# Other column order for the hidden layer, w2 loaded in four parts, conditional sums moved, first gates split

## The chip, the cores and the metric

The kernel runs on one core of one Trainium2 chip. The metric is the device time in microseconds (us) of one execution. The five instruction streams of a core are named as the profile names them: PE (TensorE, with PEld for its weight loads), DVE (VectorE), ACT (ScalarE), POOL (GpSimd) and SP (SyncE). SP computes nothing here: it reads numbers into registers and issues most of the DMAs, one after the other, in program order.

## What is computed

Chunked attention (8 batches, 8 heads, 576 positions, head size 64, chunks of 64) feeds a layer of 8 experts, of which each token uses one:

```
out   = softmax(scale * q_c @ k_c.T) @ v_c          # per chunk of 64, all float32
x     = out as (4608, 512)
xn, en = x and expert_emb, each row over its norm
p     = softmax(xn @ en.T / tau)                    # 8 experts
e     = argmax(p)
h     = relu(x @ w1[e])                             # w1: (8, 512, 1024)
y     = p[e] * (h @ w2[e])                          # w2: (8, 1024, 512)
```

## The kernel before

**Two stages.** The first 190 us or so are attention and routing, in 36 blocks of 128 tokens. Each token's row goes to a place in a DRAM table (`spots`) that is sorted by expert. The rest is the expert layer. It works in steps `j`, each on two groups of 64 tokens: group 0 comes from the experts counted upwards from 0, group 1 from the experts counted downwards from 7. So each step uses two experts at a time, and an expert is changed in one group every nine steps or so.

**One step of the expert layer.** In the loop over `j`, PE does the hidden layer of step `j + 1` (`hidden_fast`) and then the last product of step `j` (`result`, 64 matmuls with 512 columns, line 413).
- `hidden_fast` multiplies in the manner of Strassen and Winograd: seven products p1 to p7 (line 342, 16 matmuls each) into PSUM, with sums of x made by DVE (`add_x`, line 318), sums of w1 kept in `sums` (`add_up`, line 291), and DVE adding the products up in `C` (line 374). ACT applies ReLU (`relu`, line 361), DVE turns the result around in 32x32 blocks (`turn`, line 368), and that is `hT`, which `result` of the next iteration reads. PSUM has six banks for the products, taken in turn.
- The hidden layer's 1024 columns are handled as 4 blocks `r` of 256 columns `x`. Before the change `x = 8 i + k`: i (32 values) becomes the partition of `hT`, k (8 values) its slice. ReLU therefore reads with a step of 8 elements (`"p (i k) -> p k i"`) and writes contiguously. w2 lies in SBUF as `w2_rows`, with partition `p = 32 r + i` holding rows `8 p` to `8 p + 7`: 16 KB in one piece per partition.
- `hidden_plain`, with `hidden_part` (lines 253, 263, 268), is the plain product, used in the first three steps and the last one.
- `gate_parts` computes the gate of a step with small operations on ACT and DVE (lines 224 to 234); it is a generator, and each `next` issues a part.

**What SP issues in each iteration**, in this order: `load_x(j + 5)` (two register loads, then four DMAs for rows of x and two of 4 KB), `load_w2(next_of(j))` (line 177; for each group two register loads, then one DMA of 2 MB with a condition: it moves data only where the expert is a new one for that buffer), and `load_behind(j + 2)` (the same for w1, into `next_w1`). `w2` has two buffers, so `load_w2(j + 2)` waits until `result(j)` has read the buffer. A conditional DMA is issued in every iteration, whether or not it moves data, and `result` waits for it.

**Change of expert.** `take_next` (line 299) reads, for each group, a flag into a register of DVE and one of ACT; if it is set, ACT copies three quarters of `next_w1` to `w1` (line 301) and DVE makes the four sums anew (line 291). `swap_next` calls it at the end of `hidden_fast`.

The program has an order written out by hand: each engine does its instructions in the order in which the code issues them. The functions that the change touches:

Of the kernel before, what the change touches and what calls it, by code (L numbers as in the profile page):

```python
# [12 lines left out]
AF = mybir.ActivationFunctionType  # L13
# [12 lines left out]
def kernel(  # L26
# [70 lines left out]
    spot = keep.tile([P, SPOTS, MW], FP32, name="spot")  # L97

    w1_rows = moe_w1.rearrange("e (p c) f -> p e (c f)", c=KD)
    w2_rows = moe_w2.rearrange("e (p c) d -> p e (c d)", c=KF)  # L100

    src_row = keep.tile([P, NST], I32, name="src_row")

# [17 lines left out]
    def whole(w):  # L121
        return w.rearrange("p c f -> p (c f)").unsqueeze(1)

    def load_first(buf, rows):

        for s in range(2):
            e = (0, E - 1)[s]
            nc.sync.dma_start(out=whole(buf[s]), in_=rows[:, e : e + 1, :], max_dma_last_dim=4096)

# [49 lines left out]
    def load_w2(j):  # L181
        for s in range(2):
            at = of_step(s, j)
            load_when(w2_sb[s][buf_of(j)], w2_rows, eblk[at], fresh[at])

    def load_behind(j):

# [49 lines left out]
    def hidden_part(j, s, b, w1, pool, tag, ps=None):  # L237

        d = mo[j]
        if b == 0:
            if ps is None:
                ps = pool.tile([P, G // Q, KF * Q], FP32, tag=tag, name="h_ps")
            d["ps"] = ps
            if s == 0:
                d["hT"] = bp.tile([P, KF, P], FP32, tag="hT", name="hT", bufs=2)
        ps, hT = d["ps"], d["hT"]
        w = w1[s].rearrange("p c (r x) -> p c r x", r=P // Q)
        t0 = G * s + Q * b  # L250
        for c in range(KD):
            for r in range(P // Q):
                nc.tensor.matmul(
                    ps[Q * r : Q * r + Q, b],
                    lhsT=d["xT"][:, c, t0 : t0 + Q],
                    rhs=w[:, c, r],
                    start=(c == 0),
                    stop=(c == KD - 1),
                )
        if b == G // Q - 1:  # L260
            h = bp.tile([P, G // Q, KF * Q], FP32, tag="h", name="h", bufs=1)
            for b in range(G // Q):
                nc.scalar.activation(
                    h[:, b].rearrange("p (k i) -> p k i", i=Q),
                    ps[:, b].rearrange("p (i k) -> p k i", i=Q),
                    AF.Relu,
                )
            nc.vector.transpose(
                hT[:, :, G * s : G * s + G].rearrange("p k (b i) -> p b k i", i=Q),
                h.rearrange("p b (k i) -> p b k i", i=Q),  # L270
            )
# [56 lines left out]
    def hidden_fast(j, ps_h, gate, turn_next, swap_next):  # L328

        d = mo[j]  # L330
        x = quarters(d["xT"])
        s1, s2, s3, s4 = d["S"]
        W2 = KF * Q

        def product(a, m):
            ps = bank(ps_h, [P, W2])
            for c in range(KD // 2):
                for s in range(2):
                    w = block(s, m)[:, c].rearrange("p (r x) -> p r x", r=2)
                    for r in range(2):  # L340
                        t0 = G * s + Q * r
                        nc.tensor.matmul(  # L342
                            ps[t0 : t0 + Q],
                            lhsT=a[:, c, s],
                            rhs=w[:, r],
                            start=c == 0,
                            stop=c == KD // 2 - 1,
                        )
            return ps


        last = "_last" if j == LEAST - 1 else ""
        hT = bp.tile([P, KF, P], FP32, tag="hT" + last, name="hT", bufs=1 if last else 2)
        d["hT"] = hT
        C = late_p.tile([P, 4, W2], FP32, tag="C", name="C")
        U, c11, c12, c22 = (C[:, i] for i in range(4))
        h = [late_p.tile([P, 2, W2], FP32, tag=f"h{b}", name=f"h{b}") for b in range(2)]

        def relu(b, v, x):
            for s in range(2):  # L360
                nc.scalar.activation(  # L361
                    h[b][G * v : G * v + G, s].rearrange("p (k i) -> p k i", i=Q),
                    x[G * s : G * s + G].rearrange("p (i k) -> p k i", i=Q),
                    AF.Relu,
                )

        def turn(b):
            nc.vector.transpose(  # L368
                hT.rearrange("p k (s b i) -> p b s k i", b=2, i=Q)[:, b],
                h[b].rearrange("p s (k i) -> p s k i", i=Q),  # L370
            )

        def add(out, a, b, op=ALU.add):
            nc.vector.tensor_tensor(out, a, b, op)  # L374

        p1 = product(x[:, 0, 0], "B11")
        nc.scalar.copy(U, p1)
        next(gate, None)
        next(gate, None)
        p2 = product(x[:, 1, 0], "B21")  # L380
        add(c11, U, p2)
        next(gate, None)
        relu(0, 0, c11)
        turn_next()
        p3 = product(s4, "B22")
        p5 = product(s1, "T1")
        p6 = product(s2, "T2")
        add(U, U, p6)
        add(c12, U, p5)
        add(c12, c12, p3)  # L390
        relu(0, 1, c12)
        for _ in gate:
            pass
        p7 = product(s3, "T3")
        add(U, U, p7)
        add(c22, U, p5)
        relu(1, 1, c22)
        p4 = product(x[:, 1, 1], "T4")
        swap_next()
        add(U, U, p4, ALU.subtract)  # L400
        relu(1, 0, U)
        turn(0)
        turn(1)
# [42 lines left out]
    with (  # L446
# [565 lines left out]
        for t in range(-3, NT + 3):  # L1012

            if 0 <= t < NT:
                turn_a(t)
            if t == early_t - 1:
                count_early()
            if t + 3 < NT:
                turn_qk(t + 3)
                if t + 7 < NT:  # L1020
                    load_qk(t + 7)
            if 0 <= t - 2 < NT:
                logits(t - 2)
            if t - 2 in ends:
                copy_logits(ends[t - 2])
            if t == NT:
                turn_x(t - 1)
            early_parts(t, 0)
            if 0 <= t + 2 < NT:
                scores(t + 2)  # L1030
            if t - 3 in ends:
                place(ends[t - 3])
            if 0 <= t - 1 < NT - 1:
                turn_x(t - 1)
            if 0 <= t < NT:
                values(t)
                b = (2 * t + 2) // NCB + 1
                if b not in v_t and b < B:
                    load_v(b)
            if t == NT - 8:  # L1040
                load_first(w1_sb, w1_rows)
            if t == NT - 6:
                load_first([w[0] for w in w2_sb], w2_rows)
            if 0 <= t + 2 < NT:
                weights(t + 2)
            if t - 2 in ends:
                pick(ends[t - 2])
            if early_t <= t < early_t + XBUF:
                load_early(t - early_t)

            put(1 if t < NT - 2 else 2)
            if t == NT - 3:
                turn_xb(0)
                load_early(XBUF)
            if t == NT - 1:
                turn_xb(1)
            early_parts(t, 1)
            if t == -2:
                turn_experts()
            if t == -1:  # L1060
                clear_first()
# [26 lines left out]
    with (  # L1088
# [10 lines left out]
                if behind_it is not None:  # L1099
                    behind_it(s)  # L1100

        def first_parts():
            for g in first_gates:
                next(g, None)

        first_parts()
        for j in range(LEAST - 1):
            n = j + 2

            def turn_next():  # L1110
                if n < LEAST:
                    turn_xb(n)
                    if n + XBUF < NJ:
                        load_x(n + XBUF)
                    add_x(n)

            def swap_next():
                if NE <= n < LEAST:
                    take_next(n)

            if j == 0:
                first_parts()
                add_up(0, None, TS)
                first_parts()
            elif j == 1:
                turn_next()
                add_up(1, None, TS)
                hidden_plain(2, w1_sb, lambda s: add_up(s, None, ("T3",)))
            else:
                gate = gate_parts(n) if n < LEAST else iter(())  # L1130
                hidden_fast(j + 1, ps_h, gate, turn_next, swap_next)

            result(j, ps_y)
            if NE <= next_of(j) < NJ:
                load_w2(next_of(j))
            if NE - 1 <= n < LEAST - 1:
                load_behind(n)
            elif n == LEAST - 1:
                load_late(LEAST)
# [73 lines left out]
```

## Time and profile before

| | us |
|---|---|
| time, median of 3 runs (lowest to highest) | 687.28 (686.48 to 689.08) |
| the profiled execution: its time | 686.3 |
| its span, first to last instruction | 684.5 |
| PE busy | 643.0 (94%) |
| ACT busy | 441.5 (65%) |
| DVE busy | 423.5 (62%) |
| POOL busy | 160.5 (23%) |
| ReLU in `relu` (L361), 264 of 677 ns | 178.8 |
| last product (L413), 2368 matmuls | 274.4 |
| seven products (L342), 3696 matmuls | 332.8 |

The profile is of one execution; sums from it are made against its own 684.5 us. "Idle before" names the engine that ended a wait. SP has no busy time in it, since register loads and DMA issues aren't counted, so its state has to be read from the timeline and the records of its queue ("SPq"). L177 is the line of the conditional weight loads.

### The profile page before, as it was taken

Reading aid. Unit: us, or ns where it says so; the run is one execution under the profiler, and the core shown is the slowest. Engines: PE = TensorE matmul, PEld = TensorE weight load, DVE = VectorE, ACT = ScalarE, POOL = GpSimd, SP = SyncE. Lnnn points to the kernel's source line nnn. Section 1 sums busy time; section 2 is a strip of 40 time slices with the busy share of each in tenths; the row PEclk is TensorE's granted clock in tenths of the full one; section 3 lists DMA queues with packets and bytes.
Section 4 is the critical chain, followed back from the end, with each engine's and each line's share of the span. In section 5 each row is a group of like instructions: output and inputs, shape, how many; then the busy total and the mean of one; then the engine's idle time right before and its main releaser. Section 6 shows DMA issues by size and latency. Waiting matters only on the chain. (4 is left out here: it accounts for less than half of the span.)

```text
span 684.5 us, 24832 instructions
## 1 busy us (share of the span) xinstructions
PE 643.0 (94%) x9735; PEld 363.4 (53%) x9735; DVE 423.5 (62%) x1139; ACT 441.5 (65%) x767; POOL 160.5 (23%) x245
## 2 busy tenths in 40 slices
PE   6699999999998989999999999999999999999991
PEld 4599999987543434544544444344444444444430
DVE  3378888878389554556576556767655665654520
ACT  4366666655224666767787777778777677777640
POOL 8747676742241000000100100001001000001001
PEclk9799999999999999999999999999999999999996
DMA  8969998989826811111777111775821115311110
GB/s 224 262 174 243 270 263 264 265 234 337 332 96 245 323 54 44 50 47 36 283 288 287 42 49 45 276 281 204 334 79 52 39 44 189 142 38 33 49 34 30
DMA packets 92670, 112.66 MB, mean 165 GB/s; under 512 B 50316, under 2 KB 70540, under 8 KB 92536
## 3 DMA queue, kind: packets, MB, share of 16 engines
q1 hardware_dynamic: 80552, 72.32, 33.2%
q0 software_dynamic: 11952, 38.56, 17.0%
q8 instruction: 81, 1.33, 0.8%
q14 instruction: 53, 0.43, 0.2%
q10 hardware_dynamic: 32, 0.02, 0.0%
HBM read 334.71 MB, written 22.69 MB: 522 GB/s over the span
## 5 line engine op out<-in xcount | busy, mean ns | idle before, releaser
L413 PE MATMUL y_ps<-w,hT 128*32 128x512 f32 (+1 forms) x2368 | 274.4, 587 | 2.3 <-DVE C L374 2.1
L361 ACT ACTIVATE h<-C 64x256 f32<-64x256 f32 x264 | 178.8, 677 | 93.2 <-DVE C L374 68.1
L413 PEld LDWEIGHTS y_ps<-w,hT 128*32 128x32 f32 x2368 | 87.5, 110 | 159.6 <-issue 145.6
L428 POOL DMA_INDIRECT out_dram<-y,spot x36 | 34.9, 968 | 436.0 <-ACT y L421 191.4
L374 DVE TENSOR_TENSOR C<-C,h 128x256 f32<-128x256 f32 x231 | 96.1, 416 | 46.7 <-DVEq L299 39.7
L342 PE MATMUL h<-w,S 128*32 128x256 f32 x1056 | 101.1, 380 | 2.0 <-DVE w L291 2.0
L342 PE MATMUL h<-sums,xbT 128*32 128x256 f32 x1056 | 101.1, 383 | 0.0
L342 PE MATMUL h<-w,xbT 128*32 128x256 f32 x1056 | 80.7, 380 | 6.4 <-ACTq L299 5.2
L368 DVE STREAM_TRANSPOSE hT<-h 128x512 f32<-128x512 f32 x66 | 46.7, 708 | 45.4 <-ACT h L361 45.3
L342 PEld LDWEIGHTS h<-w,xbT 128*32 128x32 f32 x1056 | 40.3, 110 | 43.1 <-ACTq L299 12.8
L342 PEld LDWEIGHTS h<-w,S 128*32 128x32 f32 x1056 | 48.0, 110 | 25.2 <-DVE w L291 1.5
L342 PEld LDWEIGHTS h<-sums,xbT 128*32 128x32 f32 x1056 | 48.4, 111 | 22.5 <-issue 0.8
L680 ACT COPY xT<-tr 128x512 f32<-128x512 f32 x36 | 21.1, 585 | 53.3 <-PE tr L678 53.3
L227 DVE TENSOR_SCALAR rn<-rn 128x1 f32<-128x1 f32 x37 | 5.7, 153 | 72.8 <-ACT rn L224 72.8
L342 PE MATMUL h<-sums,S 128*32 128x256 f32 x528 | 49.9, 379 | 0.0
L789 POOL DMA_INDIRECT spots<-xr,dest x36 | 37.0, 1029 | 39.3 <-ACT aT L637 13.0
L203 DVE STREAM_TRANSPOSE xbT<-xin 128x256 f32<-128x256 f32 x73 | 44.2, 644 | 0.5 <-DVE hT L368 0.5
L224 ACT ACT_TABLE_LOAD x34 | 43.6, 1283 | 0.9 <-issue 0.4
L231 ACT ACT_TABLE_LOAD x34 | 43.6, 1283 | 0.6
L421 ACT ACTIVATE y<-y_ps,gate 128x512 f32<-128x512 f32 (+1 forms) x37 | 25.2, 682 | 29.0 <-issue 12.8
L690 PEld LDWEIGHTS rt_ps<-enT,xT 128*128 128x128 f32 x288 | 35.0, 192 | 1.1 <-issue 0.8
L570 POOL DMA_DIRECT2D kx<-in_k_dram x36 | 31.6, 881 | 16.0 <-PE tr L593 15.2
(199 smaller groups left out, 846.6 us busy)
## 6 DMA issues: line engine op xcount, KB each, us to landing
w<-in_moe_w_dram SPq DMA_DIRECT2D x74, 2048.0 KB
next_w<-in_moe_w_dram SPq DMA_DIRECT2D x67, 2048.0 KB
xin<-spots SPq DMA_DIRECT2D x158, 64.0 KB
qx<-in_q_dram POOLq DMA_DIRECT2D x32, 256.0 KB, 6.0
v<-in_v_dram SPq DMA_DIRECT2D x56, 144.0 KB
kx<-in_k_dram POOLq DMA_DIRECT2D x28, 256.0 KB, 4.3
spot<-spots SPq DMA_DIRECT2D x80, 4.0 KB
spots<-blank SPq DMA_DIRECT2D x2, 576.0 KB
```

Of the source, the lines that this page charges most:

```text
L203: nc.vector.transpose(xT[:, :, cols].rearrange("p c (b i) -> p b c i", i=Q), t[:, s * (D // 2) : (s + 1) * (D // 2)].rearrange("p (b i c) ...
L224: nc.scalar.activation(rn, spot[:, j % SPOTS, SQ : SQ + 1], AF.Sqrt)
L231: nc.scalar.activation(sh, sh, AF.Exp, accum_out=gate)
L342: nc.tensor.matmul(ps[t0 : t0 + Q], lhsT=a[:, c, s], rhs=w[:, r], start=c == 0, stop=c == KD // 2 - 1,)
L361: nc.scalar.activation(h[b][G * v : G * v + G, s].rearrange("p (k i) -> p k i", i=Q), x[G * s : G * s + G].rearrange("p (i k) -> p k i", i=Q),
L368: nc.vector.transpose(hT.rearrange("p k (s b i) -> p b s k i", b=2, i=Q)[:, b], h[b].rearrange("p s (k i) -> p s k i", i=Q),)
L374: nc.vector.tensor_tensor(out, a, b, op)
L413: nc.tensor.matmul(ps[Q * r : Q * r + Q, 0:w], lhsT=d["hT"][:, c, Q * t0 : Q * t0 + Q], rhs=w2_sb[s][buf_of(j)][:, c, d0 : d0 + w], start= ...
L428: ins = nc.gpsimd.indirect_dma_start(out=to, out_offset=bass.IndirectOffsetOnAxis(ap=at, axis=0), in_=y[:, 0:w], in_offset=None, bounds_ch ...
L570: eng.dma_start(out=x[done : done + n], in_=src[b, :, s : s + n, :].rearrange("h p d -> p h d"),)
L690: nc.tensor.matmul(rt_ps[:, batch_of[t][0] % 2, batch_of[t][1]], lhsT=d["xT"][:, c], rhs=enT[:, c], start=(c == 0), stop=(c == KD - 1),)
L789: ins = nc.gpsimd.indirect_dma_start(out=spots, out_offset=bass.IndirectOffsetOnAxis(ap=at, axis=0), in_=m, in_offset=None, bounds_check=S ...
```

## The change

1. The columns of the hidden layer are ordered `x = 32 k + i` in place of `8 i + k`. ReLU reads and writes contiguously. In `hidden_part` two calls of 256 columns become one of 512.
2. So that the rows of w2 stand in the same order, w2 is loaded otherwise: partition `32 q + i`, slice `k` holds row `256 q + 32 k + i`. One DMA of 128 partitions becomes four of 32 partitions, each with eight rows of 2 KB per partition. This holds for the first load and for `load_w2`, where each of the four DMAs has the condition.
3. In `hidden_fast`, p4 is issued straight after p7, and `swap_next` straight after p4, ahead of the two additions that use p7 and of the ReLU behind them.
4. Before, the remaining parts of the first four gates were issued together ahead of and in iteration 0. Now the first gate is finished in iteration 0, and the parts of the other three stand in iteration 1, among the sums of w1.

```diff
-    w2_rows = moe_w2.rearrange("e (p c) d -> p e (c d)", c=KF)
+    w2_rows = moe_w2.rearrange("e (q k i) d -> q i e k d", k=KF, i=Q)
...
+    def load_first_w2():
+        for s in range(2):
+            e = (0, E - 1)[s]
+            for q in range(P // Q):
+                nc.sync.dma_start(
+                    out=w2_sb[s][0][Q * q : Q * q + Q].unsqueeze(1),
+                    in_=w2_rows[q, :, e : e + 1],
+                )
...
     def load_w2(j):
         for s in range(2):
             at = of_step(s, j)
-            load_when(w2_sb[s][buf_of(j)], w2_rows, eblk[at], fresh[at])
+            e, f = number(eblk[at], E - 1, ENG.SP), number(fresh[at], 1, ENG.SP)
+            for q in range(P // Q):
+                nc.sync.dma_start(
+                    out=w2_sb[s][buf_of(j)][Q * q : Q * q + Q].unsqueeze(1),
+                    in_=w2_rows[q, :, ds(e, 1)],
+                    cond=f > 0,
+                )
...
-            for b in range(G // Q):
-                nc.scalar.activation(
-                    h[:, b].rearrange("p (k i) -> p k i", i=Q),
-                    ps[:, b].rearrange("p (i k) -> p k i", i=Q),
-                    AF.Relu,
-                )
+            nc.scalar.activation(h, ps, AF.Relu)
...
             for s in range(2):
-                nc.scalar.activation(
-                    h[b][G * v : G * v + G, s].rearrange("p (k i) -> p k i", i=Q),
-                    x[G * s : G * s + G].rearrange("p (i k) -> p k i", i=Q),
-                    AF.Relu,
-                )
+                nc.scalar.activation(h[b][G * v : G * v + G, s], x[G * s : G * s + G], AF.Relu)
...
         p7 = product(s3, "T3")
+        p4 = product(x[:, 1, 1], "T4")
+        swap_next()
         add(U, U, p7)
         add(c22, U, p5)
         relu(1, 1, c22)
-        p4 = product(x[:, 1, 1], "T4")
-        swap_next()
         add(U, U, p4, ALU.subtract)
...
-        first_parts()
         for j in range(LEAST - 1):
...
             if j == 0:
-                first_parts()
+                for _ in first_gates.pop(0):
+                    pass
                 add_up(0, None, TS)
-                first_parts()
             elif j == 1:
                 turn_next()
                 add_up(1, None, TS)
-                hidden_plain(2, w1_sb, lambda s: add_up(s, None, ("T3",)))
+                def behind_group(s):
+                    add_up(s, None, ("T3",))
+                    first_parts()
+                first_parts()
+                hidden_plain(2, w1_sb, behind_group)
```

The built program has the same matmuls in the same order as before. SP has 588 more rows (2092 against 1504 of its listed ones): for each load of w2 to one group, three more DMAs and, ahead of each, one more register operation that computes its address from expert and flag. The two register loads per group stay as they were.

More of the change, by code (lines that the diff above doesn't have):

```diff
@@ L122, in whole, with load_first_w1 @@
         return w.rearrange("p c f -> p (c f)").unsqueeze(1)
-    def load_first(buf, rows):
+    def load_first_w1():
         for s in range(2):
             e = (0, E - 1)[s]
-            nc.sync.dma_start(out=whole(buf[s]), in_=rows[:, e : e + 1, :], max_dma_last_dim=4096)
+            nc.sync.dma_start(
+                out=whole(w1_sb[s]), in_=w1_rows[:, e : e + 1, :], max_dma_last_dim=4096
+            )
[7 more added lines that the diff above has]
+                )
     xin, mo = {}, {}
@@ L183, in load_w2 @@
             at = of_step(s, j)
-            load_when(w2_sb[s][buf_of(j)], w2_rows, eblk[at], fresh[at])
+            e, f = number(eblk[at], E - 1, ENG.SP), number(fresh[at], 1, ENG.SP)
+            for q in range(P // Q):
+                nc.sync.dma_start(
+                    out=w2_sb[s][buf_of(j)][Q * q : Q * q + Q].unsqueeze(1),
+                    in_=w2_rows[q, :, ds(e, 1)],
+                    cond=f > 0,
+                )
     def load_behind(j):
@@ L1040 @@
             if t == NT - 8:
-                load_first(w1_sb, w1_rows)
+                load_first_w1()
             if t == NT - 6:
-                load_first([w[0] for w in w2_sb], w2_rows)
+                load_first_w2()
             if 0 <= t + 2 < NT:
@@ L1100, in hidden_plain, with first_parts @@
                     behind_it(s)
-        def first_parts():
-            for g in first_gates:
+        def first_parts(n=3):
+            for g in first_gates[-n:]:
                 next(g, None)
-        first_parts()
         for j in range(LEAST - 1):
```

## The prediction

> **What bounds the kernel now.** I began with the page: PE is busy for 94% of the span, and no other engine for over two thirds.
>
> ```profile
> PE 643.0 (94%) x9735; PEld 363.4 (53%) x9735; DVE 423.5 (62%) x1139; ACT 441.5 (65%) x767; POOL 160.5 (23%) x245
> ```
>
> The windows of single steps (from one start of L413 to the next) say 12.90 us where nothing disturbs, with PE busy throughout. So ACT, with 9.45 us busy in it, limits nothing there. What can be won shows in the waits of PE from 215 to 660 us:
>
> ```profile
> PE h L342 <- ACTq L299: 5.2, 6, 1.3
> PE y_ps L413 <- DVE C L374: 2.1, 1, 2.1
> PE h L342 <- DVE w L291: 2.0, 2, 1.0
> PE h L342 <- ACT w L301: 0.9, 1, 0.9
> ```
>
> That is all: 10.2 us. 6.1 us of it (first and last line) are changes of expert, where PE waits for ACT's copies. The second line is something else. The addition that it names is one for the next step's hidden layer, which L413 doesn't read. What L413 does read is w2, and SP had issued a load of it 0.2 us before PE went on at 251.14 us; SP issued the one for the other group at 252.22, and PE waited again from 252.19 to 252.32. So I read SP's timeline, around that wait and in undisturbed steps:
>
> ```profile
> 248.94 0.51 SPq L159 DMA_DIRECT2D spot<-spots  x1
> 250.93 1.36 SPq L177 DMA_DIRECT2D w<-in_moe_w_dram  x2
> ...
> 251.14 1.05 PE L413 MATMUL y_ps<-w,hT 128*32 128x512 f32 x4 [2.13 <-DVE C L374]
> ...
> 262.53 1.35 SPq L177 DMA_DIRECT2D w<-in_moe_w_dram  x2
> 265.09 1.34 SPq L177 DMA_DIRECT2D next_w<-in_moe_w_dram  x2
> 267.66 1.42 SPq L153 DMA_DIRECT2D xin<-spots  x2
> 269.32 0.51 SPq L159 DMA_DIRECT2D spot<-spots  x1
> 270.07 1.33 SPq L153 DMA_DIRECT2D xin<-spots  x2
> 271.60 0.51 SPq L159 DMA_DIRECT2D spot<-spots  x1
> 273.59 1.35 SPq L177 DMA_DIRECT2D w<-in_moe_w_dram  x2
> ```
>
> Two things are to be seen. First, PE waited for a conditional load of w2 that moved nothing: it only had to be issued. Second, SP's round, from one pair of w loads to the next, is 11.1 us (273.59 - 262.53), back to back, with register work in what look like gaps. PE's step is 12.9 us. SP, which the page doesn't show as busy, has 1.8 us to spare per step.
>
> **SP's queue: four loads for one.** What each DMA of L177 takes of SP is in that line's own records:
>
> ```profile
> L177 SPq FUSED_REGOPS  x137: 169/174/194, 211.4 to 671.9; - x137
> L177 SPq MOVE w<-in_moe_w_dram x70: 29/29/29, 211.7 to 672.1; - x70
> L177 SPq DMA_DIRECT2D w<-in_moe_w_dram x70: 73/87/416, 211.7 to 672.2; - x70
> ```
>
> A skipped one is 0.174 + 0.029 + 0.073 = 0.28 us of records. Below that it can't cost, as all of it is in order on SP. From above: two skipped loads are issued 1.28 us apart (1.35 less the second's 0.07); less the two register loads between (0.43 and 0.27) that is 0.58. In the sequence of SP's records, 0.45 us pass from the register operation at 263.48 to the next register load at 263.93, with one semaphore wait (about 0.03) that the added DMAs need not have. I take 0.43. Each iteration has six more: 6 x 0.43 = 2.6 us, so SP's round becomes 11.1 + 2.6 = 13.7 us, 0.8 us over PE's 12.9. The point at which nothing would be lost is 1.8 / 6 = 0.30 us per DMA.
>
> The loss isn't 0.8 us times the steps, since SP begins late (the wait at 251) and has other queues ahead of it. I sum its chain. From 240.96 us, when the first big loads have let SP go, to its last weight load at 672.4 there are 431.4 us, of which SP waited 50.8 (my sum of the gaps over 0.15 us between its records). Work: 380.6. Added: 34 calls of `load_w2` until there, 34 x 2.58 = 87.7. Loads that move data cost 0.32 more per DMA to issue (up to 0.416 against 0.073); 12 groups do, 12 x 3 x 0.32 = 11.5. Sum 479.8, so SP issues its last load no sooner than 240.96 + 479.8 = 720.8. Before, the span went on for 12.1 us after it, 3.5 of which SP spent waiting at the last barrier. 720.8 + 12.1 - 3.5 = 729.4 us.
>
> Who waits for this: PE at `result`, and behind it in PE's queue the next `hidden_fast`. Behind `load_w2` on SP stand `load_behind`, whose data isn't used for several steps, and `load_x`, three steps ahead; these hide their delay of at most some 20 us. `load_w2` is issued two steps ahead, so its delay is hidden up to some 15 us and then falls on PE.
>
> **The transfer itself.** 2 MB in packets of 4 KB ran at 159 ns per packet, so 16 engines x 4096 B / 159 ns = 412 GB/s, or 5.1 us. Packets of 2 KB into 32 partitions don't occur. The nearest by size is this row. The nearest by partitions are the loads of v (64 partitions, 256 B each, 18.7 ns: 219 GB/s, 9.6 us per 2 MB). Between them I take 300 GB/s, 7.0 us, as packets of 512 B (27 ns) already made 303. At the start (4 MB for step 5 from 211.7 us) that costs 2 x 1.9 = 3.8 us, as SP then stands behind a full queue (up to 9.0 at the lower rate). In the 12 later loads SP sees only what exceeds its own work: I take 0.3 us each, 3 to 4 in all, and up to 2 us each at the lower rate. Sum for this part: +7, bounds 0 and +33. [...]
>
> **ReLU.** 264 calls of 64x256 from SBUF:
>
> ```profile
> L361 ACT ACTIVATE h<-C 64x256 f32<-64x256 f32 x264 | 178.8, 677 | 93.2 <-DVE C L374 68.1 <-ACTq L299 19.2 <-DVE hT L368 3.5
> L377 ACT COPY C<-h 128x256 f32<-128x256 f32 x33 | 12.2, 369 | 3.3 <-PE h L342 3.3
> ```
>
> A contiguous call should come near the 369 ns of L377, or at most to 405 (the exponentials of 128x512 from SBUF took 620, and 256 columns are 215 less by the step from 369 to 585 in PSUM). 264 x 0.28 = 74 us off ACT. On PE this is worth nothing in plain steps. ReLU in `hidden_part` goes from two of 376 to 381 ns to one of 512 columns, about 585 (L680's copies), off the path. [...]
>
> **Conditional sums.** In the change of expert at 343.8 us, ACT's copies ran from 349.57 to 352.5, behind two pairs of ReLU (346.76 to 349.54), and PE waited 1.31 us. With one pair of 0.8 us ahead and the flags read earlier, the copies end about 1 us sooner, and DVE's sums 0.85 sooner. Against that, the additions with p7, and with them the bank of p5 and two transposes, wait for up to 4 x 1.22 us of sums. p3 of the next step needs that bank some 1.7 us after its start, about when it becomes free: 0 to 1 us each. Net gain over six changes, 3 to 6 us of PE's time. But as soon as PE waits for SP, it gains nothing at the end: the next `result` waits that much longer. I put it at 0, and the same for the first gates, which can give at most the 2.0 us of the third line of PE's waits.
>
> **Sum.** 729.4 + 7 = 736 us of span; the profiled execution's time is 1.8 over its span (686.3 against 684.5): 738 us. Its 686.3 stands 1.0 below the median, which I leave.
>
> **The rivals.**
> - *SP keeps up: faster.* If an added skipped DMA takes SP less than 0.30 us, the round stays under 12.9 us. Then `load_w2` is never late, and the gain at the changes of expert shows: 686.3 - 6.1 - 2 for the gates, +2 to 5 for SP's longer list behind the last step: about 681. For it: the bare records sum to 0.28. Against it: the gaps between SP's records are there in every round. Chance 0.10. In between, at about 0.31 to 0.34, loss and gain cancel: 0.05.
> - *Slow transfers decide: slower still.* If writing 32 partitions at a time halves the rate, PE also waits for data, above all after the one iteration in which both groups change (around 436 us) and at result(0), where the first w2 now arrives by 186 us, some 6 us ahead. 729.4 + 33 + 1.8 = 764. For it: v's rows. Against it: their packets are so small that they may be the cause. Chance 0.25.
> - *The change of expert becomes worse*, through the bank of p5: 6 x 1 us. It is hidden under SP's lateness, and doesn't stand by itself.
>
> **How the numbers follow.** Forecast (SP's round decides, time 712 to 750): chance 0.60, 738 us. The low end is 0.40 us per DMA (-6) and no stretched issues (9.5 us of SP's work are issues that waited for a full DMA queue) from 731. With the slow transfers 0.25, cancelling 0.05, faster 0.10. The range 712 to 764 leaves out faster, cancelling and a little on top. Within 0.5% (about what a measurement of this kernel can tell from no change) is 0.05, faster 0.10, slower 0.85.
>
> **What would show it.** Right: the waits of PE list L413 for some 30 to 50 us, with w loads or a stale engine as their end; SP's rounds are 13.5 to 14 us without gaps; L177's successor has about 280 w loads at 0.07 us each when skipped; L361 is near 400 ns and the total time longer all the same. Wrong: rounds of 12.9 us with waits of SP for PE at the w loads, and no wait of PE at L413. ReLU above 500 ns would make that step wrong, but not the time. Packets of 2 KB near 80 ns would put the time at 731, near 160 ns at 760.

## The result and the profile after

The changed kernel takes 772.24 us (median of 4 runs, 770.27 to 774.12) against 686.88 us: a ratio of 1.1225 with a 95% interval of 1.1188 to 1.1261. The direction was forecast, the size wasn't: 738 us was said, 764 at most. The profiled execution took 770.3 us, with a span of 768.5 us against 684.5.

Lines have moved: L423 is the last product (L413 before), L356 the seven products (L342), L375 ReLU (L361), L384 the additions (L374), L313 and L315 the change of expert (L299, L301), L166 and L172 the rows of x (L153, L159). The conditional load of w2 is L199, that of next_w1 is L190; both were L177.

The page's engine line and its group for ReLU say that ACT got shorter as meant, and the kernel longer:

```profile
PE 662.9 (86%) x9735; PEld 450.8 (59%) x9735; DVE 426.9 (56%) x1139; ACT 372.1 (48%) x760; POOL 161.2 (21%) x245
L375 ACT ACTIVATE h<-C 64x256 f32<-64x256 f32 x264 | 109.0, 413 | 151.3 <-DVE C L384 149.3
```

The waits of PE from 215 to 745 us (us in total, times, longest) were 10.2 us before:

```profile
PE y_ps L423 <- DMA w<-in_moe_w_dram: 22.3, 4, 10.4
PE h L356 <- ACT w L315: 17.6, 5, 6.3
PE y_ps L423 <- DMA spot<-spots: 9.3, 1, 9.3
PE h L356 <- DVE C L384: 6.1, 3, 2.6
PE h L272 <- DMA next_w<-in_moe_w_dram: 5.1, 1, 5.1
PE h L356 <- ACTq L313: 3.9, 4, 1.3
```

The first line is the forecast one: the last product waits for w2. The third belongs to it as well: L423 doesn't read `spot`, and 2 KB packets of w2 ran from 494.8 us to 516.1 us without a pause, just ahead of the wait that ended at 517.3. With two short ones that aren't shown, the waits at L423 come to 34 us. 11.1 us of them, around 261 us, ended when SP had issued loads that moved nothing; 20.5 us (the waits that ended at 413.4, 517.3 and 567.8) ended when packets of w2 had landed.

The second line was not forecast. ACT's copies at the changes of expert are late: they wait for the latest load of `next_w1` to be issued, even if it moves nothing. The group of these copies (idle before them, and what ended it; 1.5 us before), and one of the waits, show it:

```profile
L315 ACT COPY w<-next_w 128x1024 f32<-128x1024 f32 x18 | 17.6, 1043 | 47.1 <-DMA next_w<-in_moe_w_dram 47.1
371.44 1.37 SPq L190 DMA_DIRECT2D next_w<-in_moe_w_dram  x2
371.53 1.99 ACT L315 COPY w<-next_w 128x1024 f32<-128x1024 f32 x2 [8.62 <-DMA next_w<-in_moe_w_dram]
372.62 0.64 PE L356 MATMUL h<-w,xbT 128*32 128x256 f32 x2 [6.34 <-ACT w L315]
```

The first load of that pair took SP 0.088 us, so it moved nothing. All six such waits of ACT (47.1 us) ended within 0.1 us of the start of a load of 0.07 to 0.09 us. The load that had moved the data stood at least one iteration earlier.

So SP is late with everything. In an undisturbed stretch its timeline has this round:

```profile
288.11 3.89 SPq L199 DMA_DIRECT2D w<-in_moe_w_dram  x8
293.21 1.34 SPq L190 DMA_DIRECT2D next_w<-in_moe_w_dram  x2
295.75 1.42 SPq L166 DMA_DIRECT2D xin<-spots  x2
...
301.69 1.35 SPq L199 DMA_DIRECT2D w<-in_moe_w_dram  x4
```

301.69 - 288.11 = 13.6 us, where 13.7 was forecast (11.1 before, and PE's step is still 12.9). The records of a skipped load are those of before (minimum, median, maximum in ns), four times as many:

```profile
L199 SPq FUSED_REGOPS  x280: 169/192/198, 212.8 to 760.4; - x140
L199 SPq DMA_DIRECT2D w<-in_moe_w_dram x280: 73/73/830, 213.2 to 760.7; - x140
```

What is new stands in SP's own waits. Before, SP mostly waited for PE (241 to 673 us): it was ahead.

```profile
SPq L177 <- PE y_ps L413: 29.3, 15, 9.0
```

Now it waits for its own transfers (241 to 761 us). Its records show eight semaphores that SP's 666 DMAs take in turn (83 or 84 on each), so each DMA first waits until the one eight places earlier has landed:

```profile
SPq L166 <- DMA w<-in_moe_w_dram: 23.9, 18, 2.6
SPq L172 <- DMA w<-in_moe_w_dram: 6.6, 4, 1.9
```

Packets of 2 KB took 164 ns (median): by that 16 x 2048 B / 164 ns = 200 GB/s, where the 4 KB packets of before made 412. Counted from its first packet to its last, a load of 2 MB took 10.0 to 11.7 us, 180 to 210 GB/s.

### The profile page after: what moved, and what is told of

It reads as the page before. It is cut to its first block, busy times and chain, and to the rows that moved or that the text cites. A ratio compares the mean times of both kernels' runs of the same rounds, so it can differ in the third digit from the quotient of the medians.

```text
span 768.5 us, 25524 instructions
## 1 busy us (share of the span) xinstructions
PE 662.9 (86%) x9735; PEld 450.8 (59%) x9735; DVE 426.9 (56%) x1139; ACT 372.1 (48%) x760; POOL 161.2 (21%) x245
## 5 line engine op out<-in xcount | busy, mean ns | idle before, releaser
L423 PE MATMUL y_ps<-w,hT 128*32 128x512 f32 (+1 forms) x2368 | 281.6, 604 | 39.6 <-DMA w<-in_moe_w_dram 27.9
L423 PEld LDWEIGHTS y_ps<-w,hT 128*32 128x32 f32 x2368 | 127.6, 113 | 166.2 <-issue 118.0
L375 ACT ACTIVATE h<-C 64x256 f32<-64x256 f32 x264 | 109.0, 413 | 151.3 <-DVE C L384 149.3
L384 DVE TENSOR_TENSOR C<-C,h 128x256 f32<-128x256 f32 x231 | 96.7, 419 | 55.9 <-DVEq L313 44.3
L356 PE MATMUL h<-w,xbT 128*32 128x256 f32 x1056 | 82.5, 402 | 21.6 <-ACT w L315 17.6
L356 PE MATMUL h<-w,S 128*32 128x256 f32 x1056 | 91.7, 385 | 6.1 <-DVE C L384 6.1
L356 PE MATMUL h<-sums,xbT 128*32 128x256 f32 x1056 | 90.2, 379 | 0.0
L356 PEld LDWEIGHTS h<-w,xbT 128*32 128x32 f32 x1056 | 50.8, 115 | 51.5 <-ACT w L315 22.5
L356 PEld LDWEIGHTS h<-w,S 128*32 128x32 f32 x1056 | 52.4, 112 | 18.0 <-issue 6.1
L356 PEld LDWEIGHTS h<-sums,xbT 128*32 128x32 f32 x1056 | 52.3, 110 | 10.9
L356 PE MATMUL h<-sums,S 128*32 128x256 f32 x528 | 45.0, 379 | 0.0
L315 ACT COPY w<-next_w 128x1024 f32<-128x1024 f32 x18 | 17.6, 1043 | 47.1 <-DMA next_w<-in_moe_w_dram 47.1
```

What stands on the lines that cost most here:

```text
L356: nc.tensor.matmul(ps[t0 : t0 + Q], lhsT=a[:, c, s], rhs=w[:, r], start=c == 0, stop=c == KD // 2 - 1,)
L375: nc.scalar.activation(h[b][G * v : G * v + G, s], x[G * s : G * s + G], AF.Relu)
L423: nc.tensor.matmul(ps[Q * r : Q * r + Q, 0:w], lhsT=d["hT"][:, c, Q * t0 : Q * t0 + Q], rhs=w2_sb[s][buf_of(j)][:, c, d0 : d0 + w], start= ...
```

## How the sum is split

For each kernel I add up SP's records, as the prediction did: from its first free moment after 241 us to its last load of w2. "Waits" are gaps over 0.15 us, "full queue" what issues of over 0.8 us took beyond 0.53 us, "work" is the rest. "Full queue" is a name for these long issues and an inference: they come while packets of a big load run (7 of them before, 10 after the change); what an issue waits for, no view shows. The stretch runs from the first to the last matmul of the last product; it leaves out the first stage, which took 190 to 209 us, depending on the run. (It took 199 to 209 us on the chip that ran e7 to e14, and the ratios of those runs below hold what of it the kernel before, not profiled there, doesn't share.) All in us. (e2, e3, e7, e8 and e13 to e16 keep e1's order of the rows of w2, so their values differ as e1's do, and not the work.)

| kernel | DMAs per load, partitions | packets | work | waits | full queue | stretch |
|---|---|---|---|---|---|---|
| before | 1, all | 4 KB, 159 ns | 368.2 | 52.8 | 9.5 | 478.5 |
| e1 | 1, all | 4 KB, 159 ns | 368.0 | 50.3 | 9.6 | 474.9 |
| e7 | 2, all | 4 KB, 159 ns | 403.2 | 21.6 | 10.2 | 472.0 |
| e8 | 3, all | 4 KB, 159 ns | 438.5 | 11.5 | 11.1 | 490.2 |
| e2 | 4, all | 4 KB, 159 ns | 467.2 | 8.4 | 6.1 | 522.8 |
| e3 | 4, 32 neighbours | 4 KB, up to 334 ns | 466.7 | 40.8 | 17.6 | 564.9 |
| after | 4, 32 neighbours | 2 KB, 164 ns | 465.6 | 37.7 | 16.3 | 561.7 |
| e15 | 4, every fourth | 4 KB, 159 ns | 497.0 | 6.6 | 3.6 | 549.6 |
| e13 | 1, all | 256 B, 18 ns | 377.3 | 28.8 | 45.0 | 482.7 |
| e16 | 2, all | 256 B, 18 ns | 408.7 | 6.8 | 48.4 | 510.4 |
| e14 | 2, 64 neighbours | 4 KB, up to 334 ns | 425.6 | 36.8 | 33.1 | 526.1 |

## Experiments: the loads of w2

The first four take the changed kernel and load w2 otherwise.

**e1, one load.**

```diff
-    w2_rows = moe_w2.rearrange("e (q k i) d -> q i e k d", k=KF, i=Q)
+    w2_rows = moe_w2.rearrange("e (p c) d -> p e (c d)", c=KF)
...
-            for q in range(P // Q):
-                nc.sync.dma_start(out=w2_sb[s][buf_of(j)][Q * q : Q * q + Q].unsqueeze(1), ...)
+            load_when(w2_sb[s][buf_of(j)], w2_rows, eblk[at], fresh[at])
```

> The changed kernel with w2 loaded as before the change: one DMA of 128 partitions per group, with 16 KB per partition in packets of 4 KB. Its hidden columns keep the new order, so the rows of w2 no longer match them (the values differ; the amount of work does not). All else of the change stays. Theory A (the whole loss comes from part 2, the four DMAs): SP's round returns to 11.1 us, no wait at the last product but one near 250 us, time 676 to 684 us, as the waits at the changes of expert (6.1 us before) shrink to 1 to 4 us. Rival (the moved sums, parts 3 and 4, cost too): the waits at the changes of expert stay as long as after the change (27 us) or at least above 6, time over 690 us.

Measured: 682.72 us, ratio 0.9924 (0.9892 to 0.9956). Theory A holds: the whole loss comes from part 2. The waits for ACT at the changes of expert are gone, but 4.8 us of another kind came, which is taken up below.

**e2 and e3, four loads, wide and narrow.**

```diff
+    w2_rows = moe_w2.rearrange("e (p c) d -> p e (c d)", c=KF)     # as in e1
...
             for q in range(P // Q):
+                nc.sync.dma_start(out=part(w2_sb[s][buf_of(j)], q), in_=rows_part(q, ds(e, 1)), cond=f > 0, ...)
# e2: part q is the slices 2q and 2q + 1 of all 128 partitions
# e3: part q is all slices of the partitions 32q to 32q + 31
```

> As the kernel with one load, but each load of w2 is cut into four DMAs of two slices: each has 128 partitions and 4 KB per partition. SP issues as many DMAs as after the change; only the partitions per DMA differ. Theory A (issues and transfers add, as in the prediction's sum): SP's round is 13.6 us, packets take 159 ns, and the time is the prediction's sum without its transfer term, 729 + 2 = 731 us (725 to 737). Rival B (the slow transfers alone matter, SP's longer round is hidden): 680 to 690 us. Rival C (the number of DMAs is everything): 765 to 775 us.

> As the kernel with four wide DMAs, but each of the four has 32 partitions with all their 16 KB, in packets of 4 KB. If the 32 partitions are what halves the rate, packets of 4 KB take about 320 ns, 2 MB about 10 us, and the time is that of the changed kernel, 765 to 778 us. If instead the 2 KB packets are, packets here take 159 ns and the time is that of the four wide DMAs, about 731 us.

Measured: e2 734.86 us, ratio 1.070 (1.063 to 1.077); e3 775.50 us, ratio 1.127 (1.120 to 1.134). e2 lies on the prediction's sum without its transfer term (731), e3 on the changed kernel. So the number of DMAs costs 52 us (e2 - e1) and the narrow transfers 41 us more (e3 - e2); it isn't the 2 KB packets, as e3 has packets of 4 KB. SP's waits for its own loads tell the two apart; of e2 and of e3:

```profile
SPq L200 <- DMA w<-in_moe_w_dram: 0.9, 2, 0.4
```

```profile
SPq L167 <- DMA w<-in_moe_w_dram: 25.8, 20, 2.6
SPq L173 <- DMA w<-in_moe_w_dram: 7.1, 4, 1.9
```

**e7 and e8, two and three wide loads**: e2 with the slices cut 4 + 4 and 3 + 3 + 2.

```diff
-        return w[:, 2 * q : 2 * q + 2]...
+        return w[:, CUTS[q] : CUTS[q + 1]]...        # (0, 4, 8) or (0, 3, 6, 8)
```

> As the kernel with four wide DMAs per load, but two DMAs of four slices each (128 partitions, 8 KB per partition). Two DMAs per iteration are added instead of six. Six made SP's round 14.0 us against 11.1, 0.48 us each. Theory A (a threshold at PE's 12.9 us): SP's round is 12.1 us, the added issues are hidden, and the time is that of the kernel with one load, 680 to 686 us. Rival (every added DMA costs time: 52 us for six per iteration, 8.7 for each): 700 us.

> Three wide DMAs per load (three, three and two slices of 128 partitions): four DMAs per iteration are added. Theory A (a threshold): SP's round is 12.8 to 13.0 us, as long as PE's step; the lateness of the start and of the loads that move data is then never made up, but hardly grows: 688 to 702 us. Rival (8.7 us for each): 717 us.

Measured: e7 ratio 0.9956 (0.9929 to 0.9983), e8 1.0205 (1.0159 to 1.0251). The kernel before took 695.14 us on this chip, so ratios are compared. 8.7 us for each added DMA would give ratios of 1.018 and 1.043: refuted. There is a threshold. SP's undisturbed round was 12.1 to 12.3 us in e7, 12.8 to 13.2 in e8 and 13.7 to 14.2 in e2, with PE's step at 12.9. e8 came out at the slow end of its range (702 us on the scale of 687); its stretch is 15 us over e1's.

**e15, every fourth partition.** Four DMAs of 32 partitions and packets of 4 KB, as e3; only which partitions differs.

```diff
-        return whole(w[Q * q : Q * q + Q])
+        return w.rearrange("(i a) c d -> a i (c d)", a=4)[q].unsqueeze(1)
```

> As the kernel with four narrow DMAs (32 neighbouring partitions each, packets of 4 KB, 775 us), but each of the four has every fourth partition (0, 4, 8 and so on). Number of DMAs, partitions, bytes and packets are the same; only which partitions differs. If the slow rate comes from the number of partitions, packets stay at 334 ns and the ratio at 1.126. [...]

Measured: ratio 1.1062 (1.1021 to 1.1103), between e2's 1.070 and e3's 1.127. Packets took 159 ns (10% and median; 172 at 90%), and SP's waits and full queue fell to 6.6 and 3.6 us: the transfers are as fast as wide ones. What is left over e2 is SP's own work, 497 us against 467. A DMA with spaced partitions takes it longer to issue, 124 ns where nothing is moved, against 73:

```profile
L200 SPq DMA_DIRECT2D w<-in_moe_w_dram x280: 124/124/870, 210.0 to 748.8; - x140
```

The skipped and the taken ones together make 25 of the 30 us (29.6 + 30.5 us in this line against 17.0 + 17.9 in e2). So neighbours are what halves the rate, not the number of partitions. Side by side: 32 neighbours make 180 to 210 GB/s from first packet to last, 64 neighbours in e14 take the same 334 ns per packet of 4 KB as 32, every fourth partition takes 159 ns, as all 128 do. Why neighbours are slower, no run shows.

**e14, e13 and e16, the slow rate with fewer DMAs.** e14 has two DMAs of 64 neighbouring partitions. e13 and e16 are e1 and e7 with packets cut to 256 B, which make 227 GB/s in all partitions (16 x 256 B / 18.0 ns); from first packet to last their loads took 8.0 to 10.5 us.

```diff
# e14
-            for q in range(P // Q):
+            for q in range(2):
...
+        return whole(w[G * q : G * q + G])          # G = 64
# e13, e16: the loads of w2 alone
-            max_dma_last_dim=4096
+            max_dma_last_dim=256
```

> Two DMAs per load, each of 64 partitions with all their 16 KB in packets of 4 KB; its issues are those of the kernel with two wide DMAs (ratio 0.996). If the rate goes with the number of partitions up to 128, packets take some 210 to 240 ns and 2 MB 7 us; if 64 partitions have what 128 have, 159 ns and the ratio of the two wide DMAs, 0.99 to 1.00; if they are as slow as 32, 320 ns, and the time tells what slow transfers cost beside an SP with 0.8 us to spare: theory A 1.00 to 1.03, the rival 1.05.

> The kernel with one load of 128 partitions per group, whose packets are cut to 256 B, so that 2 MB takes about the 10 us of the narrow loads (v's packets of 256 B make 219 GB/s), with one DMA to issue. Theory A (SP with time to spare hides slow transfers): ratio 1.00 to 1.02, what is lost being at the start. Rival (slow transfers cost 38 us whatever SP has to spare): ratio 1.05. If the packets aren't that slow, it tells nothing.

> Two wide DMAs per load (four slices of 128 partitions), with packets cut to 256 B: the rate of narrow loads, the issues of the kernel with two DMAs, no neighbouring partitions. Two DMAs of 64 neighbours took 526 us from the first to the last product of the second stage, two wide ones of 4 KB 472, one of 256 B 483. Theory (a slow load costs what SP cannot make up afterwards, 0.8 us per step here against 1.8 with one DMA): near the two halves, 510 to 530 us of that stretch. Rival (it is the narrowness itself, by what it does to other transfers): near the one load of 256 B, 480 to 495.

Measured: e14 ratio 1.0819 (1.0789 to 1.0849), over what either side had said; e13 1.0172 (1.0149 to 1.0196); e16 1.0475 (1.0437 to 1.0512), its stretch of 510 us at the low end of the theory's range. With slow transfers in place of fast ones, the stretch grew by 8 us with one DMA (e13 over e1), 38 with two (e16 over e7), 42 with four (e3 over e2), and 54 with two of 64 neighbours (e14 over e7). The table says why e13 is cheap: SP lost 35 us more to full queues, but had 50 us of waits to lose, mostly for PE as before, and 29 were left. In e16 hardly any were (7). So theory A's cushion, SP's spare time per step, is real. It isn't everything: e14 has the same cushion as e16 (both are e7 with slower transfers), and costs 16 us more. Its loads are slower: about 10.5 us for 2 MB against 9.1 on average in e16, some 20 us over 14 loads (an estimate from these two numbers). No run sets the two to one rate, so whether the neighbouring partitions cost anything beyond it stays open.

**e11 and e12, next_w1 loaded by another engine.** The changed kernel, with `load_behind` issued by ACT and by POOL, which takes 2.5 us out of SP's round.

```diff
-            load_when(next_w1[s], w1_rows, after[at], more_e[at])
+            load_when(next_w1[s], w1_rows, after[at], more_e[at], ENG.Activation, nc.scalar)   # e12: ENG.Pool, nc.gpsimd
```

> The changed kernel, with its four DMAs of 32 partitions, but the loads of next_w1 and their register loads are issued by ACT in its own queue in place of SP: 2.5 us less in SP's round, so 11.1 us. ACT has 3 to 5 us per step to spare. Theory A (the slow transfers cost much only because SP is over PE's step; SP with time to spare makes up for them): 688 to 705 us, with waits of PE left at the start and where both groups change. Rival (the slow transfers cost their 38 us whatever SP has to spare): 720 to 725 us.

> The changed kernel, but the loads of next_w1 and their register loads are issued by POOL in place of SP (ACT's queue in the run before shared its DMA semaphores with SP's, and SP waited 105 us for them). SP's round then needs 11.1 us. Theory A (narrow transfers cost much only where SP has no time to spare): ratio to the kernel before 1.00 to 1.03, with waits of PE at the start and after the iteration in which both groups change. Rival (the slow transfers cost their 38 us in any case): ratio 1.05 or more. If POOL's loads land late, waits of ACT's copies for next_w show it, as in the changed kernel (47 us).

Measured: e11 ratio 1.1414 (1.1367 to 1.1461), no faster than the change itself (its stretch is 564.2 us). It tells nothing of the theories, since ACT's loads use the same eight semaphores. SP now waited for loads that ACT issued late; e11's waits of SP:

```profile
SPq L166 <- DMA next_w<-in_moe_w_dram: 105.5, 19, 21.2
```

e12: 1.0707 (1.0678 to 1.0736), with SP's undisturbed round back at 11.1 us. Its stretch is 516.6 us, so it wins 45 of the 83 us back, not all of them, and is on the rival's side: the slow transfers cost much even where SP has time to spare. SP still waited 37.9 us, from 205 us on, for loads of w2 at L166 and L172; four of the eight semaphores are held by one load there. No run changes the number of semaphores alone.

## Experiments: the three small parts

**e9, the moved sums alone**: the kernel before, with part 3 of the diff and nothing else.

> The kernel before with part 3 alone: p4 straight after p7, and the conditional copies and sums ahead of the two additions with p7. ReLU keeps its step of 8 (677 ns), w2 its one DMA, the gates their place. The waits for ACT at changes of expert (6.1 us) should shrink to 1 to 3 us, and waits for the bank of p5 of some 5 us come in their place, as in the kernel with one load: ratio 0.995 to 1.001. If ReLU's shortening carries the gain of that kernel (0.992), more of the waits for ACT stay here than there (none); if the moved sums do, none stay.

Measured: ratio 1.0135 (1.0107 to 1.0164), which was not expected. Its waits of PE from 215 us on:

```profile
PE h L342 <- ACTq L299: 5.2, 4, 1.3
PE h L342 <- DVE C L374: 4.3, 6, 2.2
PE h L342 <- ACT w L301: 1.0, 1, 1.0
```

That is 10.5 us against 10.2 before, and the stretch is 480.2 against 478.5. Moving the sums brought nothing where ReLU was slow: the waits for ACT stayed, and the bank of p5 came on top. Most of the rest must lie in the first stage, which the edit doesn't touch: the first matmul of L413 came at 208.0 us, against 190 to 193 in every profile of two other chips and 199 to 209 in the other seven of this one. The kernel before was not profiled on this chip, and what makes the first stage differ there stays open.

**e17, contiguous ReLU alone.** w2's partition p, slice k holds row 128 k + p, which one DMA of all partitions loads. The columns of w1 are then read in runs of 32 or 64. Sums and gates stand as before.

```diff
+    w2_rows = moe_w2.rearrange("e (k p) d -> p e k d", k=KF)
...
+        w = w1[s].rearrange("p c (k r i) -> p c r k i", k=KF, i=Q)
...
+        return (w1 or w1_sb)[s].rearrange("p (u c) (k v x) -> p u v c k x", u=2, v=2, k=KF)[:, u, v]
```

> The kernel before with part 1 alone, through the version in which rows of w2 stand 128 apart and one DMA of 128 partitions loads them: ReLU contiguous, conditional sums and gates where they were. ReLU takes 413 ns. If the 5 us of gain come from the moved sums, the waits for ACT at the changes of expert stay near 6 us and the ratio is 0.998 to 1.002. If the shorter ReLU ahead of the copies carries it (two pairs of 0.26 us less at each of six changes, 3 us), those waits fall to about 3 us, without waits for the bank of p5, and the ratio is 0.994 to 0.998.

Measured: 680.91 us, ratio 0.9907 (0.9877 to 0.9937). Its waits of PE from 215 us on:

```profile
PE y_ps L411 <- DMA w<-in_moe_w_dram: 2.9, 1, 2.9
PE h L344 <- DVE w L293: 2.1, 2, 1.1
PE h L344 <- ACT w L303: 0.3, 1, 0.3
PE h L344 <- ACTq L301: 0.2, 1, 0.2
```

The waits for ACT at the changes of expert fell from 6.1 to 0.5 us. The shorter ReLU does that by itself.

**e6, the same with the moved sums and the split gates.**

> A version with ReLU contiguous and one DMA per group: partition p, slice k of w2 holds row 128 k + p, which one DMA with 128 partitions and packets of 2 KB can load. The columns of w1 are then read in eight runs of 32 (by PE) or 64 (by ACT and DVE). All else as after the change. If partitions set the rate, 2 KB packets take near 80 ns and the time is that of the kernel with one load, 676 to 684 us. If 2 KB packets are slow by themselves, they take about 160 ns here too: 683 to 695 us, since SP has time to wait. If reading w1 in runs costs PE anything, products at over 384 ns each show it; at 5% it would be 16 us.

Measured: 683.55 us, ratio 0.9938 (0.9906 to 0.9969). Packets of 2 KB into all partitions took 84 ns, so they aren't slow by themselves; products stayed at 379 ns, so reading w1 in runs costs PE nothing. e1 and e6 have the same new wait; of e1:

```profile
PE h L343 <- DVE C L371: 4.8, 4, 2.7
```

p3 of the next step waits for the PSUM bank of p5, because the addition that frees it stands behind the conditional sums.

**e10, the change of expert split**: e6 with ACT's copies behind the ReLU of c12 and DVE's sums behind the two additions with p7.

```diff
         relu(0, 1, c12)
+        swap_next(take_copies)
...
-        swap_next()
         add(U, U, p7)
         add(c22, U, p5)
+        swap_next(take_sums)
```

> The version with rows of w2 apart and one DMA per group, in which the change of expert is split: ACT's conditional copies stand behind the ReLU of c12 (their places in w1 are free after p3), and DVE's conditional sums behind the two additions with p7, so that the bank of p5 comes free before them. Theory: the 4.8 us that PE waits for the bank of p5 at four changes go, and nothing new comes: 683.6 - 4.8, so 677 to 681 us. Rival (ACT's copies, now ahead, delay the copy of p1 or the ReLU and so the sums): the waits move to L315's successor or to C, time 682 to 688 us.

Measured: ratio 0.9837 (0.9801 to 0.9873), the fastest version. From 215 us on PE waits 1.1 us in all:

```profile
PE h L348 <- ACT C L379: 0.8, 2, 0.6
PE y_ps L416 <- DVE S L324: 0.3, 1, 0.3
```

**b2, the kernel before once more**, to see whether it has the long first stage too.

> The kernel before once more, for its profile on this chip: the part of the program ahead of the second stage took 192 us on one chip and 200 to 208 in the later runs, although nothing in it was changed. If this is the chip, it shows here too; the ratio is 1.00.

Measured: ratio 1.0021 (0.9996 to 1.0047), first matmul of L413 at 190.1 us, stretch 478.8. This was another chip than that of e9, so it doesn't settle e9's first stage. It shows that two profiles of one kernel agree to 0.3 us in the stretch.

## Why the prediction was wrong by 34 us

- **SP's work: right.** Forecast were 87.7 + 11.5 = 99.2 us of added work. In e2, which has the issues without the narrowness, it is 467.2 - 368.2 = 99.0. The last load was said for 720.8 us; in e2 it came at 723.4, and the span is 730.9 where 729.4 was summed. That the sum is so close is luck in part: SP's waits before are 52.8 us, not the 50.8 taken, and e2 has 8.4 us of waits that the sum put at nothing, and 3.4 us less of full queue. e7 and e8 lie on either side of the threshold as forecast.
- **The transfer term: the step that failed.** It said +7, with bounds of 0 and +33. Between e2 and the changed kernel, SP's waits grew by 29.3 us and its full queue by 10.2: 39.5, of which 37.6 show in the span (768.5 - 730.9). Two things were mis-sized. The rate taken was 300 GB/s and is 200 by the packets' time, 180 to 210 from first packet to last; the rows of v (219) were the right end. That was luck in part: packets of 256 B make 227 in all partitions too (e13), so v's rate needn't come from its 64 partitions. And "SP sees only what exceeds its own work" (0.3 us per load) overlooked that a DMA waits for the one eight places before it: SP stood behind its own landings for 30.5 us. The start cost 8.8 us (the first loads behind it were issued at 260.1 us, in e2 at 251.3), where 3.8 was said and 9.0 at most. The 12 later loads cost the other 28.5 us (the last load at 760.7, in e2 at 723.4), 2.4 us each, where 0.3 was said and 2 at most. So even the upper bound was too low.
- **load_behind and load_x "hide their delay"**: wrong for `load_behind`. Its data isn't used for several steps, but the copies wait for the latest load to be issued, as the prediction had itself read it for w2: PE waited 17.6 us for such copies and 5.1 us for a load of next_w1 in the last steps. This lies beside SP's lateness and adds nothing to the sum: SP waited for PE only 0.5 us in all, so its chain alone sets the end (241.0 + 519.6 + 7.8 = 768.4).
- **ReLU: the duration nearly (413 ns, at most 405 said), its worth wrong.** "On PE this is worth nothing in plain steps" is true, but the changes of expert aren't plain steps: e17 gains 5.6 us there.
- **Conditional sums: wrong by themselves.** A gain of 3 to 6 us was credited to them. Alone they gained none (e9), beside the short ReLU they cost 4.8 us (e1). That price is the rival's "bank of p5", said as 6 us. That all of it is hidden behind SP was right.
- **First gates**: 2.0 us of waits (L291) became 1.8 (1.0 and 0.8 in e1).
- **The rivals.** "SP keeps up" needed under 0.30 us per skipped DMA; it is 0.43. "Slow transfers decide", 764 us, was the true case, and deserved more than 0.25. The trace of before couldn't show 32 partitions, but its nearest row by partitions, v's (9.6 us per 2 MB by its rate; 10.0 to 11.7 measured), was the end of the range to take.
- **What would show it.** The waits at L423 are 34 us (30 to 50 said), the rounds 13.6 to 14.0, 280 loads at 0.07 us: all as said. "2 KB packets near 160 ns" came true as well, and 760 was said for it.

## What to carry to other kernels

Splitting a conditional load costs the issuing queue on every pass, whether or not data moves (0.43 us per added DMA here): set the added issues against the queue's spare time per step, which no engine line shows. And ask where each piece lands: a load of 32 or 64 neighbouring partitions runs at half rate here (packets of 4 KB 334 ns against 159), and its landing holds up whatever reuses its semaphore (30.5 us of SP's waits here). Before a layout is paid for with more DMAs, look for one that a single DMA can load; rows 128 apart gave the contiguous ReLU for nothing (e17, ratio 0.9907).

## What was not expected of the hardware

After a wait of PE of 5 to 10 us its granted clock was 0.83 to 0.88 for a step, in three such steps. Windows of the changed kernel around a wait of 6.15 us (561.7 to 567.8; columns as in the profile: PE, PEld, DVE, ACT and POOL busy, granted clock, DMA share, GB/s):

```profile
548.60:567.80 19.20, 13.09 (x180) 6.74 (x172) 12.52 (x36) 10.21 (x24) 0.97 (x1) 0.94 0.80 219
567.80:583.00 15.20, 15.16 (x176) 11.00 (x180) 3.42 (x11) 5.27 (x11) 0.97 (x1) 0.85 0.11 34
583.00:596.00 13.00, 13.00 (x184) 10.04 (x180) 7.35 (x22) 7.34 (x15) 0.97 (x1) 1.00 0.14 43
```

The step behind it took 15.2 us with PE busy throughout, the next one 13.0. (The other two: 0.88 behind the wait of 10.4 us that ended at 261.6, 0.83 behind the one of 5.1 us that ended at 413.4.) In all PE was busy 19.9 us longer than before (662.9 against 643.0) for the same matmuls. Here that lies beside SP's lateness; where PE sets the end, such a wait would cost about 2.3 us more than its length (an estimate from these windows: 15.2 - 12.9).
